# Attention and SwiGLU on one core: matrix pieces in a stored order, no order between the two banks of a PSUM tile, and a rearranged start

## The chip, the cores and the metric

The kernel runs on one core of one Trainium2 chip. The metric is device time in microseconds (us), with the reference's inputs.

Engines: PE multiplies matrices (PEld is its weight load), DVE is VectorE, ACT is ScalarE, POOL is GpSimd, SP issues most DMA. PE writes into PSUM; a PSUM bank holds 512 fp32 per partition. "Half clock" is time in which the profile shows that PE was granted half of its clock. A load "lands" when its data has arrived.

## The reference, cut to what matters

```python
# attention: 8 batches x 8 heads, 576 positions, head size 64; causal, with a decay
decay = cum[:, :, :, None] - cum[:, :, None, :]           # cum = cumsum(log(clip(f)))
scores = np.where(causal, -1e9, q @ k.T / sqrt(64) + decay)
x = softmax(scores) @ v                                   # -> 4608 tokens x 512
# feed-forward on all tokens
xn = x / sqrt(mean(x * x) + 1e-6) * rms_g
g = xn @ w_gate                                           # 512 -> 1536
out = (g * sigmoid(g) * (xn @ w_val)) @ w_out             # 1536 -> 512, fp32
```

## The kernel before

The kernel cuts all work into pieces and has a planner in Python that decides, while the program is built, in which order each engine does its pieces. The program itself is static: on the chip, each engine takes its instructions in that order and waits on semaphores. On PE the pieces are, with the letters used below: T turns queries and keys, S and L are scores, V multiplies by values, X turns the normalised result (d, once, turns the decay); then, for a group of 512 tokens, 12 gates G, 12 values U, and 8 output products P. A G and its U are four matmuls of 512 columns each, a P is six.

Before, the planner picked PE's next piece by a greedy rule:

```python
def choose(cands):                                # cuts marked by ...
    ffn = [c for c in cands if c[2].name[0] in "GUP"]
    att = sorted((c for c in cands if c[2].name[0] not in "GUP"), key=...)
    late = u + LEAD(u) - done["att"] / att_us     # how far attention is to run ahead
    ...
# a gate is made to follow the piece before it, so G and U alternate:
add(("G", g, fc), "PE", 0.87, ..., own + [("w", fc // 4 * 2)] + ([last] if last else []), [bg, ("xT", g)])
add(("U", g, fc), "PE", 0.87, ..., [("G", g, fc), ...], [bg, ("xT", g)])
last = ("U", g, fc)
```

G and U share one PSUM tile of two banks. Three such tiles (`bufs=3`) serve the scores, the G/U pairs and the outputs. ACT takes tanh of bank 0, DVE multiplies twice:

```python
def gate(g, fc):
    bg = bgs[g, fc] = ps_b.tile([128, 2, GT], F32, name="bg")
    ... nc.tensor.matmul(bg[:, 0, :], lhsT=wg[...], rhs=xTs[g][:, dc, :], ...)
def gate_tanh(g, fc):
    readers[g, fc] = [nc.scalar.activation(ths[g, fc], bgs[g, fc][:, 0, :], ACT.Tanh, scale=0.5)]
def value(g, fc):
    ... mm = nc.tensor.matmul(bgs[g, fc][:, 1, :], lhsT=wv[...], ...)
        beside(mm, readers.get((g, fc), ()))      # no dependency on readers of bank 0 that stand before it
```

The framework tracks dependencies by tile, not by bank. `beside` frees a value matmul from a tanh emitted before it. It doesn't free a tanh that is emitted after the value matmul: that tanh waits for a bank it doesn't read.

The softmax here doesn't subtract the row's maximum and nothing guards it: scores larger than these inputs give would overflow.

## Time and profile before

| | before |
|---|---|
| time, median of 4 | 441.9 us (441.7 to 446.0) |
| profiled run, span | 442.8 us |
| PE busy | 387.9 us, 88% |
| half clock | 17.1 us in three stretches |

Lines of the page of the kernel before: the busy times; then PE, ACT, granted PE clock and DMA in 40 equal slices (a digit is tenths).

```profile
PE 387.9 (88%) x3267; PEld 207.4 (47%) x3317; DVE 263.0 (59%) x545; ACT 216.9 (49%) x364; POOL 171.3 (39%) x358
...
PE   1756888879999799999999998998898999999996
...
ACT  3564644455546833675575347454682351332322
...
PEclk9986999988999999999999999999999999999999
DMA  9999999899436703583237030200011001102002
```

PE looks nearly full, but its row counts overlapped and stretched time too. I use another account: for each two neighbouring matmuls, the distance of their starts minus the distance that undisturbed ones of that size have in this trace (216 ns at 512 columns, 56 ns at 128, 29 ns at 65). What is over is lost. The undisturbed distances alone sum to 356 us.

The waits view of PE before (who waited for whom: total us, times, longest us):

```profile
PE tr L308 <- DVE qkb L286: 8.8, 3, 7.7
PE bg L575 <- ACT PT L362: 5.3, 10, 0.9
PE bg L357 <- DVE QK L314: 4.4, 7, 2.0
PE bg L442 <- DVE xn L433: 4.2, 1, 4.2
PE po L395 <- ACT PT L338: 3.8, 9, 0.8
PE po L395 <- POOL PT L323: 3.3, 5, 1.8
PE po L395 <- DVE x L406: 2.7, 5, 0.6
```

The first (the start) and fourth (the first normalisation) are single long waits. The others are many short ones: a gate (L575) that waits for an exp (L362) to free a PSUM tile, scores that wait for a QK copy, value products that wait for exps, masks and copies.

The line of the tanh in the groups view (busy us, mean ns of one | idle before it, and who ended the idle time):

```profile
L580 ACT ACTIVATE th<-bg 128x512 f32<-128x512 f32 x108 | 64.4, 597 | 120.5 <-PE bg L590 103.5 <-PE bg L575 11.7 <-PE po L334 2.3
```

L590 is the value matmul. And in the timeline (start us, duration, engine, line):

```profile
156.03 1.03 PE L575 MATMUL bg<-xT,wg 128*128 128x512 bf16 x4
...
156.89 1.03 PE L590 MATMUL bg<-xT,wv 128*128 128x512 bf16 x4
...
157.75 1.03 PE L575 MATMUL bg<-xT,wg 128*128 128x512 bf16 x4
...
157.96 0.60 ACT L580 ACTIVATE th<-bg 128x512 f32<-128x512 f32 x1 [1.13 <-PE bg L590]
```

The gate ends at 157.06 us, its value at 157.92 us, and the tanh, which reads the gate alone, starts at 157.96 us.

### The profile page before, as it was taken

Reading aid. Unit: us, or ns where it says so; the run is one execution under the profiler, and the core shown is the slowest. Engines: PE = TensorE matmul, PEld = TensorE weight load, DVE = VectorE, ACT = ScalarE, POOL = GpSimd, SP = SyncE. Lnnn points to the kernel's source line nnn. Section 1 sums busy time; section 2 is a strip of 40 time slices with the busy share of each in tenths; the row PEclk is TensorE's granted clock in tenths of the full one; section 3 lists DMA queues with packets and bytes.
Section 4 is the critical chain, followed back from the end, with each engine's and each line's share of the span. In section 5 each row is a group of like instructions: output and inputs, shape, how many; then the busy total and the mean of one; then the engine's idle time right before and its main releaser. Section 6 shows DMA issues by size and latency. Waiting matters only on the chain.

```text
span 442.8 us, 8567 instructions
## 1 busy us (share of the span) xinstructions
PE 387.9 (88%) x3267; PEld 207.4 (47%) x3317; DVE 263.0 (59%) x545; ACT 216.9 (49%) x364; POOL 171.3 (39%) x358
## 2 busy tenths in 40 slices
PE   1756888879999799999999998998898999999996
PEld 1443444545445445554545554544444444444442
DVE  5754666255763587566755784666553873670770
ACT  3564644455546833675575347454682351332322
POOL 2848545796429703862274148332330010000000
PEclk9986999988999999999999999999999999999999
DMA  9999999899436703583237030200011001102002
GB/s 158 205 198 200 202 206 212 153 248 205 90 73 155 191 1 73 143 204 73 64 83 199 1 73 2 95 2 2 1 48 49 1 0 49 48 1 80 16 0 96
DMA packets 123658, 43.19 MB, mean 98 GB/s; under 512 B 114272, under 2 KB 118880, under 8 KB 123616
## 3 DMA queue, kind: packets, MB, share of 16 engines
q1 hardware_dynamic: 118784, 37.65, 38.9%
q0 software_dynamic: 4832, 4.98, 6.8%
q8 instruction: 26, 0.43, 0.4%
q14 instruction: 16, 0.13, 0.1%
HBM read 37.90 MB, written 9.44 MB: 107 GB/s over the span
## 4 chain that ended last, share of the span: by engine, by line
PE 62%; DVE 12%; ACT 7%; DMA 5%; issue 5%; SPq 4%; POOL 4%; ACTq 0%; POOLq 0%; DVEq 0%
PE bg L575 18%; PE bg L590 17%; PE bg L606 17%; DMA v<-in_v_dram 5%; PE po L395 4%; SPq L182 4%; DVE th L584 3%; DVE hT L596 3%; DVE x L406 2%; PE bg L357 2%; ACT th L580 2%; ACT PT L362 2%; PE tr L442 2%; PE tr L308 1%; DVE xn L433 1%
## 5 line engine op out<-in xcount | busy, mean ns | idle before, releaser
L580 ACT ACTIVATE th<-bg 128x512 f32<-128x512 f32 x108 | 64.4, 597 | 120.5 <-PE bg L590 103.5
L584 DVE SCALAR_TENSOR_TENSOR th<-th,bg 128x512 f32<-128x512 f32 x108 | 74.2, 687 | 82.1 <-ACT th L580 79.4
L575 PE MATMUL bg<-xT,wg 128*128 128x512 bf16 x414 | 110.0, 381 | 8.4 <-ACT PT L362 5.3
L590 PE MATMUL bg<-xT,wv 128*128 128x512 bf16 x416 | 108.3, 379 | 0.9 <-issue 0.2
L362 ACT ACTIVATE PT<-bg 128x1024 bf16<-128x1024 f32 x96 | 93.6, 1024 | 26.0 <-PE bg L357 21.8
L606 PE MATMUL bg<-wo,hT 128*128 128x512 bf16 x416 | 97.7, 379 | 3.7 <-DVE hT L596 1.5
L323 POOL TENSOR_SCALAR_AFFINE_SELECT PT<-PT 128x256 bf16<-128x256 bf16 (+2 forms) x128 | 56.4, 450 | 73.1 <-ACT PT L362 43.6
L596 DVE SCALAR_TENSOR_TENSOR hT<-th,bg 128x512 bf16<-128x512 f32 x108 | 74.1, 686 | 5.7 <-PE bg L590 2.3
L575 PEld LDWEIGHTS <-wg 128*128 128x128 bf16 x432 | 41.2, 98 | 52.9 <-issue 11.1
L606 PEld LDWEIGHTS <-hT 128*128 128x128 bf16 x432 | 40.5, 98 | 48.1 <-issue 4.6
L590 PEld LDWEIGHTS <-wv 128*128 128x128 bf16 x432 | 40.9, 98 | 46.2 <-issue 1.0
L395 PEld LDWEIGHTS <-PT 128*128 128x128 bf16 x960 | 38.4, 101 | 22.3 <-issue 8.0
L395 PE MATMUL po<-Vs,PT 128*128 128x65 bf16 x900 | 39.9, 197 | 10.0 <-ACT PT L338 3.8
L614 ACT COPY ores<-bg 128x512 f32<-128x512 f32 x36 | 20.9, 586 | 48.3 <-PE bg L606 45.1
L357 PE MATMUL bg<-QK 64*128 64x64 bf16 (+3 forms) x576 | 33.1, 247 | 6.9 <-DVE QK L314 4.4
L314 DVE COPY QK<-tr 128x640 bf16<-128x640 bf16 (+1 forms) x64 | 28.9, 452 | 16.9 <-PE tr L308 15.7
L308 PE MATMUL tr<-ident,qkb 128*128 128x128 bf16 x288 | 28.1, 228 | 10.0 <-DVE qkb L286 8.8
L286 POOL CAST qkb<-q 128x512 bf16<-128x512 f32 x28 | 17.2, 615 | 46.8 <-PE tr L308 43.8
L293 POOL TENSOR_TENSOR Vs<-v,decT 128x512 bf16<-128x512 f32 x30 | 31.5, 1062 | 0.8 <-DMA v<-in_v_dram 0.6
L406 DVE TENSOR_TENSOR x<-po,rden 128x320 f32<-128x320 f32 x60 | 29.5, 492 | 2.1
L308 PEld LDWEIGHTS <-qkb 128*128 128x128 bf16 x288 | 20.0, 101 | 20.8 <-DVE qkb L286 9.8
L462 DVE TENSOR_SCALAR xT<-tr,rg 128x448 bf16<-128x448 bf16 (+7 forms) x58 | 18.4, 358 | 18.3 <-PE tr L442 18.2
(63 smaller groups left out, 232.5 us busy)
## 6 DMA issues: line engine op xcount, KB each, us to landing
out_dram<-ores SPq DMA_DIRECT2D x36, 256.0 KB, 2.0
q<-in_q_dram SPq DMA_DIRECT2D x64, 128.0 KB, 3.4
v<-in_v_dram SPq DMA_DIRECT2D x64, 128.0 KB, 3.5
k<-in_k_dram SPq DMA_DIRECT2D x62, 128.0 KB, 3.5
wg<-in_moe_w_gate_dram POOLq DMA_DIRECT2D x3, 512.0 KB, 6.7
wv<-in_moe_w_val_dram POOLq DMA_DIRECT2D x3, 512.0 KB, 9.3
wo<-in_moe_w_out_dram POOLq DMA_DIRECT2D x2, 768.0 KB, 10.5
r<-in_q_dram SPq DMA_DIRECT2D x8, 128.0 KB, 3.9
```

The lines of the kernel that those rows point to most:

```text
L308: nc.tensor.transpose(tp[:, (c - c0) * 128:(c - c0 + 1) * 128], src[:, c, :, :].rearrange("p h d -> p (h d)"), ident)
L323: nc.gpsimd.affine_select(out=d, in_=d, pattern=pattern, compare_op=ALU.is_ge, fill=0.0, base=0, channel_multiplier=-1)
L357: nc.tensor.matmul(sc[:, par, c:c + m], lhsT=QK[n][rows, KEYS[kj]:KEYS[kj] + 128], rhs=QK[n][rows, q0:q0 + m], start=True, stop=True)
L362: nc.scalar.activation(t[:, bank, :, :], bgs.pop((n, bank, "s")), ACT.Exp, scale=scale)
L395: mm = nc.tensor.matmul(po[:, qi, :], lhsT=weights_of(n, par, qi, kj), rhs=Vs[b % 2][:, kj, h, :], start=(kj == 0), stop=(kj == qi))
L406: nc.vector.tensor_tensor(x[:, :, h * D:(h + 1) * D], po[:, :, 0:D], bcast(r[:, :], D), ALU.mult))
L575: nc.tensor.matmul(bg[:, 0, :], lhsT=wg[:, dc, fc * 128:(fc + 1) * 128], rhs=xTs[g][:, dc, :], start=(dc == 0), stop=(dc == NDC - 1))
L580: readers[g, fc] = [nc.scalar.activation(ths[g, fc], bgs[g, fc][:, 0, :], ACT.Tanh, scale=0.5)]
L584: readers[g, fc] += [nc.vector.scalar_tensor_tensor(t, in0=t, scalar=1.0, in1=bgs[g, fc][:, 0, :], op0=ALU.add, op1=ALU.mult)]
L590: mm = nc.tensor.matmul(pv, lhsT=wv[:, dc, fc * 128:(fc + 1) * 128], rhs=xTs[g][:, dc, :], start=(dc == 0), stop=(dc == NDC - 1))
L596: nc.vector.scalar_tensor_tensor(hT, in0=ths.pop((g, fc)), scalar=0.5, in1=bgs.pop((g, fc))[:, 1, :], op0=ALU.mult, op1=ALU.mult)
L606: mm = nc.tensor.matmul(po, lhsT=hTs[g, fc][:, j * 128:(j + 1) * 128], rhs=wo[:, fc, :], start=(fc == 0), stop=(fc == NFC - 1))
```

## The change

Its intent: an order of PE's pieces found beforehand and stored as a string; the two banks of a tile made independent in both directions; a start with the first loads earlier and the exp table (what ACT loads before its first exp) fetched while DVE works. The core of the diff (`...` marks cuts):

```diff
+ORDER = "".join("""
+TTSTSSTdTLSTSSLTVTSSVSSLVVSLSVVVTVTXXXXSTGXUGGLUUTGUSGXUTGVTULSV
+... (7 lines cut)
+GUUGPPUPGPUGUGGGUUUPPPPPPPP
+""".split())
...
-        plan.run(choose, rank, count)
+        plan.run([queues[c].pop(0) for c in ORDER])
...
-    def beside(mm, others):
-        for other in others:
-            tc.declare_no_dep(mm.ins, other.ins, reason="another part")
+    def in_bank(tile, bank, *instructions):
+        for ins in instructions:
+            seen = banks.setdefault(tile, [])
+            for other_bank, other in seen:
+                if other_bank != bank and other.ins.engine != ins.ins.engine:
+                    tc.declare_no_dep(ins.ins, other.ins, reason="another bank")
+            seen.append((bank, ins))
...
-                own + [("w", fc // 4 * 2)] + ([last] if last else []), [bg, ("xT", g)])
+                own + [("w", fc // 4 * 2)], [bg, ("xT", g)])
...
+    NHT = NFC + 6                      # hidden buffers: 18, were NFC + 2 = 14
-    START_W = (14.0, 14.0, 27.5, 28.0, 36.0, 37.0, 44.0, 46.0)
+    START_W = (14.0, 14.0, 24.0, 25.0, 32.0, 33.0, 42.0, 44.0)
...
+    add("ident_f", "POOL", 1.3, rows_of_one, behind=("ld", 0, "k"))      # identity after the first key loads
+    add("tables", "ACT", 1.5, lambda: nc.scalar.activation(spare, mhalf[0:1, 0:1], ACT.Exp), ["log", "ident_f"])
+    add("gains", "SP", 0.6, load_gains, dma=0.1, behind=("ld", 3, "v"))  # gains (rms_g) later
```

The durations that the planner assumes for the other engines are renewed as well (tanh 0.63 us, was 0.60; DVE's multiply 0.72, was 0.69, and so on). They order DVE, ACT, POOL and SP around the fixed order on PE. The freedom of the banks is legal on the chip: the Trainium skill, "PSUM — Partial Sum Buffer", section "PSUM bank collisions raise a hardware error", says that two engines on different banks run clean.

## The prediction

> **What bounds the kernel now.** TensorE is busy 388 of 442.8 us (busy table), but its own work is smaller. With the start-to-start spacing of undisturbed matmuls in the trace (216 ns at 512 columns, 56 ns at 128; the Trainium skill, "TensorE: Matmul & The Clock Gate", section "Wait — 56ns, not 53.3ns?", gives 215.7 and 55.6, and the trace agrees), all pieces add up to an estimated 358 us. The other 85 us: 7.7 before the first matmul, 3.9 after the last, and time lost between matmuls: 22 us up to 40 us, 17 from 40 to 100, 40 from 100 to 380, 0.4 after that (timeline of PE). About 4.4 us of it is half clock, three stretches after idle gaps. So ordering and latency bound it, not an engine's limit: DVE is busy 59%, ACT 49%. DMA is saturated until about 82 us.
>
> **What the change does.** Matmul work is unchanged.
> 1. No order between the banks. Before, the value matmuls are emitted ahead of the tanh that reads the other bank, so tanh waits for them: the groups view gives 120 us idle before tanh, 103 released by value matmuls; the median tanh starts 0.90 us after its gate's last matmul, where one 4-matmul piece takes 0.86. After, 0.05 to 0.2 us. ACT runs in order, so exps behind it, and the PSUM buffers they free, come earlier too. FFN alone (380 to 440 us) lost only 0.4 us, so this pays only in the mixed stretch.
> 2. Stored order: attention runs further ahead (batch 1's products end at PE work 39 us, not 47; batch 2's at 80, not 87; estimates), gates run two ahead, output products are split among transposes, with 18 instead of 14 hidden buffers. This attacks the 40 us of waits spread thinly over exp, QK copies, x copies and hT.
> 3. Start: key loads before the identity, gains later, exp table (1.28 us) off the decay chain. First matmul 1 to 1.5 us earlier.
>
> **How much is critical.** Loads limit the early part: two batches (estimated 15.3 us each, from landings 0.6 us apart) and all weights (estimated 29 us) can't be in before about 61 us; batch 2's last queries and keys landed at 79 us, and the new order needs them at PE work 52 us, so at least 27 us are lost by there (before: 45). Savings, estimated: start 4 us, 40 to 100 us 7, 100 to 380 us 15 (40 to 25). Tail unchanged (eight output products end both orders).
>
> **Prediction:** 416 us, 8 in 10 between 406 and 429. Faster by over 2%: 0.92; within 2%: 0.07; slower: 0.01.
>
> **What would show it.** First matmul near 6.5 us; tanh idle released by gate rather than value matmuls, median start under 0.3 us after the gate; matmul spacing unchanged; PE busy about 375 us, its share 90% or more; lost time in the mixed stretch near 25 us; nothing gained in the last 60 us; DMA bytes equal.
>
> **What would make it wrong.** A fixed order stalls PE on whatever comes late: if batch 2's transposes stand before their loads land, PE stands with gates ready behind them, and the early gain vanishes. If two gates ahead hold all three PSUM buffers, scores wait. If DVE's pair (0.69 us twice per 1.73 us of gate and value) ends the waits rather than tanh, bank freedom gives little. If the stored order fits the chip better than I allow, it goes to 405.

## The result, and the profile after

| | before | after |
|---|---|---|
| time, median | 441.9 us | 414.3 us (413.1 to 415.5, 4 runs) |
| ratio of fast runs | | 0.935, 95% interval 0.930 to 0.941 |
| profiled run, span | 442.8 us | 411.4 us |
| PE busy | 387.9 us, 88% | 381.6 us, 93% |
| half clock | 17.1 us in three stretches | 17.1 us in two stretches |

A ratio is the mean time of one kernel's fast runs over that of the other's in the same rounds, so it isn't quite the ratio of the medians.

The same lines of the page after:

```profile
PE 381.6 (93%) x3317; PEld 204.5 (50%) x3317; DVE 263.6 (64%) x545; ACT 216.8 (53%) x365; POOL 171.9 (42%) x358
...
PE   0784977999999999999999999999999999999996
...
ACT  4575553776357644746786447744754443323221
...
PEclk9996995999999999999999999999999999999999
DMA  9999999999876531646364400200020002001002
```

From the eighth slice on PE is full. In the first four slices PE does no more than before (19 tenths of a slice in both; a slice is 11.1 us before and 10.3 us after), and in the sixth and seventh it falls to 7; the clock's dip in the seventh slice (62 to 72 us) is new. The account of lost time, worked out from the two traces as told above (us of PE time in each stretch):

```
stretch (us)      before   after
before first matmul  7.7     7.3
0 to 40             22.4    22.0
40 to 100           16.0    14.2
100 to 380          36.6     7.8
380 to the end       0.0     0.0
after last matmul    3.9     3.9
sum                 86.6    55.2      difference 31.4 = 442.8 - 411.4
```

The traces' 50 missing matmul records of the kernel before are filled in here. The stretches of the prediction (22, 17, 40) are some 4 to 5 us larger in sum; it seems that it counted a part of the missing records as lost time. With its two ends and the 0.4 us they come to 91 us, not to the 85 us that it names.

So nearly all of the gain comes from the mixed stretch, where attention and feed-forward share PE. All the lines of the waits view of PE after:

```profile
PE tr L326 <- DVE qkb L304: 9.4, 4, 7.3
PE tr L326 <- DVE QK L332: 5.8, 3, 4.4
PE tr L326 <- POOL qkb L304: 2.6, 1, 2.6
PE po L416 <- POOL PT L341: 2.3, 1, 2.3
PE tr L326 <- DVE qkb L301: 1.7, 1, 1.7
PE bg L465 <- DVE xn L456: 1.2, 1, 1.2
PE bg L378 <- DVE x L427: 0.9, 2, 0.5
PE bg L606 <- DVE hT L629: 0.8, 1, 0.8
PE bg L378 <- DVE QK L332: 0.5, 1, 0.5
PE po L416 <- DVE x L427: 0.4, 1, 0.4
```

The many short waits are gone; no gate waits for an exp any more. The tanh's line and a piece of the timeline (L606 is the gate now, L622 the value, L612 the tanh):

```profile
L612 ACT ACTIVATE th<-bg 128x512 f32<-128x512 f32 x108 | 64.5, 598 | 79.6 <-PE bg L606 79.4
```

```profile
155.86 1.89 PE L606 MATMUL bg<-xT,wg 128*128 128x512 bf16 x8
...
157.59 1.03 PE L622 MATMUL bg<-xT,wv 128*128 128x512 bf16 x4
...
157.79 0.60 ACT L612 ACTIVATE th<-bg 128x512 f32<-128x512 f32 x1 [0.27 <-PE bg L606]
```

Here two gates stand in a row (x8), and the second one's tanh starts at 157.79 us, 0.04 us after the gate's end, while the value runs. The median of all 108 tanh is 0.04 us after the gate's last matmul; it was 0.90 us.

What is left between 55 and 70 us is long waits. In the timeline after:

```profile
58.10 0.24 PE L416 MATMUL po<-Vs,PT 128*128 128x65 bf16 x2
...
58.74 1.06 POOL L311 TENSOR_TENSOR Vs<-v,decT 128x512 bf16<-128x512 f32 x1 [3.64 <-DMA v<-in_v_dram]
...
60.69 1.05 PE L416 MATMUL po<-Vs,PT 128*128 128x65 bf16 x13 [2.35 <-POOL PT L341]
...
61.55 1.90 PE L606 MATMUL bg<-xT,wg 128*128 128x512 bf16 x4
...
65.41 0.61 POOL L304 CAST qkb<-q 128x512 bf16<-128x512 f32 x1 [3.95 <-DMA q<-in_q_dram]
...
66.07 0.96 PE L326 MATMUL tr<-ident,qkb 128*128 128x128 bf16 x5 [2.63 <-POOL qkb L304]
```

POOL waits for the last values of batch 1 and for the first queries of batch 2; PE stands behind POOL, in its fixed order. Four gate matmuls take 1.90 us in place of 1.03 us: from 61.1 us on PE had half its clock for 10.2 us.

### The profile page after: what moved, and what is told of

Same layout as the page of the kernel before. It is cut to its first block, busy times and chain, and to the rows that moved or that the text cites. A ratio compares the mean times of both kernels' runs of the same rounds, so it can differ in the third digit from the quotient of the medians.

```text
span 411.4 us, 8714 instructions
## 1 busy us (share of the span) xinstructions
PE 381.6 (93%) x3317; PEld 204.5 (50%) x3317; DVE 263.6 (64%) x545; ACT 216.8 (53%) x365; POOL 171.9 (42%) x358
## 2 busy tenths in 40 slices
DMA packets 123658, 43.19 MB, mean 105 GB/s; under 512 B 114272, under 2 KB 118880, under 8 KB 123616
## 4 chain that ended last, share of the span: by engine, by line
PE 87%; DVE 4%; DMA 4%; SPq 2%; issue 1%; POOL 1%; ACT 0%; DVEq 0%; POOLq 0%; ACTq 0%
PE bg L622 22%; PE bg L639 22%; PE bg L606 22%; PE po L416 7%; PE bg L378 6%; PE tr L326 4%; DMA r<-in_k_dram 3%; PE tr L465 2%; SPq L196 1%; SPq L192 1%; DMA q<-in_q_dram 1%; DVE xn L456 1%; DVE x L427 1%; DVE junk_DVE L440 1%; DVE qkb L304 1%
## 5 line engine op out<-in xcount | busy, mean ns | idle before, releaser
L606 PE MATMUL bg<-xT,wg 128*128 128x512 bf16 x432 | 108.5, 382 | 0.8 <-DVE hT L629 0.8
L622 PE MATMUL bg<-xT,wv 128*128 128x512 bf16 x432 | 107.0, 381 | 0.0
L612 ACT ACTIVATE th<-bg 128x512 f32<-128x512 f32 x108 | 64.5, 598 | 79.6 <-PE bg L606 79.4
L639 PE MATMUL bg<-wo,hT 128*128 128x512 bf16 x432 | 101.5, 379 | 0.0
L629 DVE SCALAR_TENSOR_TENSOR hT<-th,bg 128x512 bf16<-128x512 f32 x108 | 72.5, 684 | 16.3 <-PE bg L622 9.4
L622 PEld LDWEIGHTS <-wv 128*128 128x128 bf16 x432 | 40.6, 98 | 44.9 <-issue 1.2
L606 PEld LDWEIGHTS <-wg 128*128 128x128 bf16 x432 | 40.3, 98 | 45.4 <-issue 2.5
L326 PE MATMUL tr<-ident,qkb 128*128 128x128 bf16 x288 | 29.6, 234 | 19.5 <-DVE qkb L304 9.4
L416 PEld LDWEIGHTS <-PT 128*128 128x128 bf16 x960 | 37.2, 99 | 12.4 <-POOL PT L341 2.7
L332 DVE COPY QK<-tr 128x640 bf16<-128x640 bf16 x64 | 29.0, 453 | 21.8 <-PE tr L326 16.4
L416 PE MATMUL po<-Vs,PT 128*128 128x65 bf16 x900 | 38.7, 196 | 2.8 <-POOL PT L341 2.3
L326 PEld LDWEIGHTS <-qkb 128*128 128x128 bf16 x288 | 20.9, 103 | 32.1 <-DVE qkb L304 10.2
```

The source lines that it names most:

```text
L326: nc.tensor.transpose(tp[:, (c - c0) * 128:(c - c0 + 1) * 128], src[:, c, :, :].rearrange("p h d -> p (h d)"), ident)
L416: mm = nc.tensor.matmul(po[:, qi, :], lhsT=weights_of(n, par, qi, kj), rhs=Vs[b % 2][:, kj, h, :], start=(kj == 0), stop=(kj == qi))
L606: mm = nc.tensor.matmul(bg[:, 0, :], lhsT=wg[:, dc, fc * 128:(fc + 1) * 128], rhs=xTs[g][:, dc, :], start=(dc == 0), stop=(dc == NDC - 1))
L612: in_bank(("bg", "f", g, fc), 0, nc.scalar.activation(ths[g, fc], bgs[g, fc][:, 0, :], ACT.Tanh, scale=0.5))
L622: mm = nc.tensor.matmul(pv, lhsT=wv[:, dc, fc * 128:(fc + 1) * 128], rhs=xTs[g][:, dc, :], start=(dc == 0), stop=(dc == NDC - 1))
L629: nc.vector.scalar_tensor_tensor(hT, in0=ths.pop((g, fc)), scalar=0.5, in1=bgs.pop((g, fc))[:, 1, :], op0=ALU.mult, op1=ALU.mult))
```

## The experiments

Twelve kernels ran. All outputs are right. The first four split the gain. Theory: the order is most of it. Rival: the freedom of the banks is.

### The old rule for the banks, in the stored order

```diff
-                if other_bank != bank and other.ins.engine != ins.ins.engine:
+                if other_bank != bank and other.ins.engine != ins.ins.engine \
+                        and ins.ins.engine == mybir.EngineType.PE and tile[1] != "x":
```

> The changed kernel, with the old rule for the banks (only a matmul that follows a reader of the other bank is free of it; a reader that follows a matmul of the other bank waits). In the stored order only 30 of 108 tanh stand behind their own value matmuls, in the old order 88. Theory (the order is most of it, and running gates ahead already avoids the wait): 415 to 421 us, under 2% lost. Rival (freedom of the banks is the main part): 425 us or more.

Measured: 425.3 us, ratio to the kernel before 0.957 (0.950 to 0.964). The instructions stand in the same order; only waits differ. Free banks are worth 11 us in the stored order: more than the theory allowed, and at the edge of what the rival had forecast (425 us or more). The tanh's line shows what came back:

```profile
L612 ACT ACTIVATE th<-bg 128x512 f32<-128x512 f32 x108 | 64.5, 597 | 94.2 <-PE bg L606 55.2 <-PE bg L622 37.5 <-DVE hT L629 1.4
```

A part of the idle time, 37.5 us, is again released by value matmuls. These are the waits of 30 of the 108 tanh, as many as the text above counts behind their own value matmuls.

### The old order on PE, with the rest of the change

```diff
-ORDER = (the stored order)
+ORDER = (the letters of the kernel before, in 9 lines)
+    queues["T"][0:2] = queues["T"][1::-1]      # keys of the first pair first, as before
```

> The changed kernel with exactly the old order of the pieces on PE; the free banks, the 18 hidden buffers, the new start and the new durations stay. Theory: 430 to 440 us, most of the gain is lost. Rival (free banks): 415 to 424 us.

Measured: 436.2 us, ratio 0.984 (0.978 to 0.989). The order, with what the planner makes of the other engines around it, is worth 22 us. As an account of most of the gain the rival falls: with free banks the tanh is on time here too (median 0.04 us after the gate), and still 22 of the 28 us are missing. Of the first two runs, one went to each side.

### The old order and the old rule for the banks

The two edits above together.

> The changed kernel with the old order on PE and the old rule for the banks; what is left of the change is its start, the buffers and the durations that order the other engines. Both theories: 438 to 444 us, near the kernel before. If it is under 434, the rest of the change is worth more than I think. The difference to order_old is what free banks are worth in the old order: theory 2 to 8 us, rival 15 us or more.

Measured: 449.6 us, ratio 1.014 (1.008 to 1.019), 13.4 us above the run with the old order and free banks. So in the old order free banks are worth 13 us, between the two theories' figures. It is also some 7 us slower than the kernel before, which neither theory expected. What differs from it is the start, the renewed durations and earlier weight loads, which order the other engines, and the 18 buffers. In the account of lost time the excess is in the mixed stretch (41.2 us, 36.6 before). Which of these parts costs it stays open.

### Gates not ahead of values

In the stored order, the places of G and U are kept but alternate again:

```diff
-GTUTSVGTLSUVSXGTVULSVXGVGTLGVUUUPTPSTPP...
+(the same places, each G followed by its U)
```

> The changed kernel with the same stored order, except that among the places of gates and values they alternate again (gate, its value, next gate), so that no gate runs ahead; free banks stay. Theory that running gates ahead is a large part of the gain: 422 to 432 us. Rival, that attention running ahead and the split output products are the gain: under 419 us.

Measured: 425.9 us, ratio 0.961 (0.954 to 0.968). Letting gates run ahead, with the other engines' order that comes with it, is worth 11.6 us in this order, with free banks; the mixed stretch loses 19.3 us in place of 7.8. (The planner orders the other engines around PE's order, so theirs moved too, and the two shares aren't separated. This holds for every run that changes PE's order.)

### Later loads of the output weights, first try

The next two ask why the early part gained so little. The output weights were issued at 50 and 51 us and landed at 60 and 65 us, though the first output product starts at 82 us; the queries of batch 2 landed at 62 and 65 us.

```diff
-    START_W = (14.0, 14.0, 24.0, 25.0, 32.0, 33.0, 42.0, 44.0)
+    START_W = (14.0, 14.0, 24.0, 25.0, 32.0, 33.0, 58.0, 62.0)
```

> The changed kernel with the two loads of the output weights issued later (their earliest times in the plan 58 and 62 us, not 42 and 44); nothing else. In the changed kernel they were issued at 50 and 51 us, landed at 60 and 65 us and were first needed at 82 us, while the queries of batch 2, issued from 47 us, landed only at 62 and 65 us, and PE stood 2.4 us and 4.5 us between 58 and 66 us and then ran at half clock for 10.2 us. Theory (the weight loads take the bandwidth of those queries): the queries land near 56 to 58 us, the stall before the transposes of batch 2 and most of the half clock go, 405 to 410 us. Rival (the loads of queries are late anyway, or the time is lost again later): 412 us or more.

(The 4.5 us in this text is a misreading, and so is the 6.9 us in a text further below: the two waits between 58 and 66 us are 2.4 and 2.6 us, 5.0 us together.) Measured: 422.7 us, ratio 0.955 (0.953 to 0.958): 8 us slower than the changed kernel, against the theory. This wait is new in it:

```profile
PE bg L639 <- DMA wo<-in_moe_w_out_dram: 4.4, 2, 3.6
```

It was a badly made test. The planner's 58 and 62 us became 70 and 75 us on the chip, the weights landed at 80 and 85 us, and output products waited. From 60 to 80 us, where the theory spoke, this kernel lost 2.9 us (7.7 in the changed kernel); from 80 to 100 us it lost 12.9 (1.9).

### Later loads of the last third of gate and value weights too

```diff
+    START_W = (14.0, 14.0, 24.0, 25.0, 46.0, 48.0, 60.0, 64.0)
```

> As the run before, and the last third of gate and value weights later too (46 and 48 us in the plan, not 32 and 33; they landed at 51 and 55 us and were first needed at 72 and 73 us), so that the values of batch 1 (landed at 55 and 59 us; their scaling ended the 2.4 us stall) come earlier as well. Theory: 402 to 408 us, below the run before. Rival: gates wait for their weights, or nothing changes: as the run before or slower.

Measured: 420.9 us, ratio 0.953 (0.949 to 0.956). The same fault: output weights landed at 75 and 81 us, with 5.5 us of waits on them.

### The parts of the start undone

```diff
+    rows_of_one()                               # identity before the key loads
+    with nc.allow_non_contiguous_dma(reason="512 gains, once"):
+        nc.sync.dma_start(out=rg, in_=moe_rms_g.rearrange("(c p) -> p c", p=128))
-    add("tables", "ACT", 1.5, lambda: nc.scalar.activation(spare, mhalf[0:1, 0:1], ACT.Exp), ...)
+    add("tables", "ACT", 1.5, lambda: None, ...)
     (the ops "ident_f" and "gains" keep their place in the plan and emit nothing)
```

> The changed kernel with the three parts of the start undone: identity before the key loads, gains loaded first, exp table not fetched ahead. The times of the plan are left, so that the other engines keep their order. Theory, from the trace: first matmul came only 0.35 us earlier and the first gate 1.1 us later than in the kernel before, so the start is worth at most 1 us: 413.5 to 416 us. Rival (the prediction's 4 us at the start): 417 to 419 us.

Measured: 413.9 us (409.6 to 415.1, 6 runs), ratio 0.934 (0.931 to 0.938), the same as the changed kernel. The new start is worth nothing.

### Keys first on PE

```diff
+    queues["T"][0:2] = queues["T"][1::-1]
```

> The changed kernel with the first two pieces swapped on PE: keys turned before queries, as the kernel before had it. DVE casts the keys first (6.17 us), but the stored order makes PE wait for the queries (7.35 us), and the fifth query piece waits till 9.64 us. Theory: first matmul near 6.7 us, first scores 0.5 to 1 us earlier, 0.5 to 1.5 us less in all if the start is a chain; else the same as the changed kernel within 0.5 us.

Measured: 416.0 us, ratio 0.940 (0.938 to 0.943). The first matmul came at 6.95 us and the first value products at 19.1 us in place of 20.8 us, but the first gate at 40.7 us, where it was 40.6. The gain of 1.7 us was gone again within the first batch. The text above expected a gain or the same time; that the run is 1.7 us slower is within the overlap of the two intervals. The last values of batch 1 landed at 60 and 64 us, not 55 and 59; the second third of the gate and value weights was issued earlier (at 31 and 34 us, not 36 and 39), since the planner had reordered POOL too. So the swap wasn't tested alone.

### The output weights moved, and nothing else

This repeats the failed test in a clean way: the plan is untouched, and two DMA instructions are issued later in POOL's stream.

```diff
+    MOVED = {("W", 7): 6, ("C", 8, 0): 7}       # after this piece of POOL: load weights 6, 7
...
             op.emit()
+            self.then(op.name)                  # issues the moved load
...
-        add(("w", i), "POOL", 1.0, lambda i=i: load_w(i) if i < 6 else load_wo(i - 6), ...)
+        add(("w", i), "POOL", 1.0, (lambda: None) if i in MOVED.values() else lambda i=i: ..., ...)
```

> wo_late was a bad test: by its trace the loads of the output weights were issued at 70 and 75 us, landed at 80 and 85 us, and PE waited for them (4.4 us), while up to 80 us it had done more work than the changed kernel (40.3 against 38.7 us); and a later time in the plan also reordered VectorE, ScalarE and GpSimd. Here the plan is kept as it is, and only these two loads are issued later in the stream of GpSimd: after the scaling of the last values of batch 1 and after the first query cast of batch 2. By the order of instructions nothing else moves. Theory (the weight loads delay the queries of batch 2): issued near 57 to 59 us, landing before 70 us, first needed after 74 us; the stalls between 58 and 66 us fall from 6.9 us to under 3 us, and 407 to 411 us in all. Rival (late loads are not what holds the early part): 413 us or more.

Measured: 409.6 us (406.3 to 412.2, 6 runs), ratio 0.925 (0.921 to 0.929). In its timeline the queries of batch 2 are cast at 59.16 us, not at 65.41 us, without a wait, and PE turns them without one:

```profile
59.16 0.61 POOL L307 CAST qkb<-q 128x512 bf16<-128x512 f32 x1
...
60.87 0.44 PE L329 MATMUL tr<-ident,qkb 128*128 128x128 bf16 x5
```

The queries landed at 54 and 56 us, the output weights at 65 and 71 us, before the first product at 75 us. The half clock from 61 us is gone, and 60 to 80 us loses 2.1 us in place of 7.7.

That the place of the two loads is worth some 5 us is shown by the times: nothing else was moved, and the slowest of these six runs is faster than the fastest of the changed kernel (412.2 against 413.1 us). That they cost it by holding up the queries is not shown. The queries were issued at 44.2 and 44.8 us here, and at 47.2 and 50.4 us in the changed kernel. The first of these differences can't come from the edit, since the changed kernel issues its first output weights only at 49.8 us:

```profile
47.19 4.26 SPq L192 DMA_DIRECT2D q<-in_q_dram  x2
...
49.83 0.89 POOL L220 DMA_DIRECT2D wo<-in_moe_w_out_dram  x1
```

And the trace of the run with the start undone, whose output weights stand in the old place (issued at 51.3 and 52.5 us), has the same cast at the same time, without a wait, and no half clock from 61 us either; its queries were issued at 44.4 and 47.1 us and landed at 56.1 and 56.7 us:

```profile
59.21 0.61 POOL L307 CAST qkb<-q 128x512 bf16<-128x512 f32 x1
```

Both traces are of the fastest of six runs (406.3 and 409.6 us; medians 409.6 and 413.9). So early queries come without the edit too, and one trace of each kernel can't tell how much of the picture is the edit's.

### The last gate and value weights moved as well

```diff
+    MOVED = {("C", 7, 0): 4, ("m", 5, 0): 5, ("W", 7): 6, ("C", 8, 0): 7}
```

> As the run before, and the last gate and value weights are also moved in the stream of GpSimd, to about 48 and 51 us (issued at 42.8 and 44.1 us in the changed kernel, first needed at 72 and 73 us). Theory: the values of batch 1 land before 56 us and the 2.4 us stall on their scaling goes too: 405 to 409 us, 1 to 3 us under the run before. Rival: gates or values now wait for these weights, or no difference.

Measured: 406.8 us (405.1 to 408.6, 6 runs), ratio 0.919 (0.917 to 0.922). This is the best kernel: 8.1% under the kernel before. The values of batch 1 land at 50 us. From 60 to 80 us its trace loses about 5 us, more than the trace of the run before, so single traces don't carry this comparison. Whether it beats the run before is within the spread of both.

### Free banks alone, in the kernel before

The function `in_bank` and its calls for gates, values and outputs, put into the kernel before. The order of instructions is the same on every engine.

```diff
         readers[g, fc] = [nc.scalar.activation(ths[g, fc], bgs[g, fc][:, 0, :], ACT.Tanh, scale=0.5)]
+        in_bank(("bg", "f", g, fc), 0, *readers[g, fc])
...
-            beside(mm, readers.get((g, fc), ()))
+            in_bank(("bg", "f", g, fc), 1, mm)
```

> The kernel before with only the new rule for the banks of gate, value and output tiles; by the order of instructions every engine's order is as before, only waits are gone. From order_old against both_old (436.2 and 449.6 us), free banks are worth 3% in the old order: theory 427 to 433 us, the tanh's idle time released by value matmuls gone. Rival (the 13 us there came from the new durations together with the banks): 436 us or more.

Measured: 429.0 us, ratio 0.969 (0.966 to 0.972): 13 us from removed waits alone. The tanh's line:

```profile
L591 ACT ACTIVATE th<-bg 128x512 f32<-128x512 f32 x108 | 64.5, 597 | 100.3 <-PE bg L585 96.3 <-PE po L344 1.9 <-DVE hT L610 1.6
```

The release has gone from value to gate matmuls (L585). No gate waits for an exp in it any more (5.3 us, 10 times, in the kernel before). The mixed stretch loses 25.7 us, where it lost 36.6.

### Output products together

The eight P of each group are put at the place of the first; all else of the stored order stays.

```diff
-...GTLGVUUUPTPSTPPTSTVSXPTPXPLXSVXPVSG...
+...GTLGVUUUPPPPPPPPTSTTSTVSXTXLXSVXVSG...
```

> The changed kernel with the eight output products of each group put together at the place of the first, the rest of the stored order unchanged: no attention piece and no gate stands between them. The run with alternating gates lost 11.6 us of the order's 22 us. Theory: the mixing with products is the rest, because the turned x and QK copies and exps of attention need time between pieces that only long products give: 420 to 430 us. Rival: mixing is worth nothing, and the rest is attention running ahead: under 418 us.

Measured: 444.3 us, ratio 1.008 (1.001 to 1.015). Both theories missed: this costs 30 us, more than the whole order is worth over the old one. The wait with the largest sum in it is new:

```profile
PE tr L465 <- DVE xT L487: 10.5, 15, 0.7
```

Turned pieces go through one PSUM tile (`ps_tr`, `bufs=1`). When they stand side by side, each waits for DVE to empty it; between two long products the copy is hidden. The kernel before mixed its products with attention too, so this shows that the mixing must not be lost, not what the stored order adds to it. The values of single features of an order don't add up. That attention runs further ahead, which the prediction named as well, was not tested by itself.

## Why the prediction was right or wrong

The predicted 416 us lie close to the measured 414.3 us, but this is partly luck: the sum is right with terms that are not. The mixed stretch gave 14 us more than forecast, the start and the early part 8 us less.

- **What bounds the kernel: right.** Waits and order, not an engine. PE's matmul spacing was unchanged (216 ns), and removing waits alone in the kernel before gave 3%.
- **Free banks: right in mechanism.** The tanh moved from 0.90 to 0.04 us after the gate, released by gates, and the gain lies in the mixed stretch. It is worth 13 us in the old order and 11 us in the stored one. The prediction gave no separate figure.
- **The mixed stretch, "15 (40 to 25)": the term was mis-sized.** It gave 29 us (36.6 to 7.8). I had taken 25 of 40 us to remain; cut to 100 to 380 us, the waits view after is empty; before, it had waits of a gate for an exp (2.9 us, 7 times) and sixteen more lines there.
- **"Start 4": wrong.** It gave 0.4 us before the first matmul and another 0.4 us up to 40 us, and undoing the three parts changed nothing. First, the stored order makes PE wait for queries while DVE casts keys first, so the first matmul came at 7.35 us, not 6.5. Second, an earlier start wasn't passed on: keys first brought the first value products 1.7 us forward and the first gate not at all.
- **"40 to 100 us 7": mis-sized.** It gave 1.8 us. What the prediction had named as its first risk happened: transposes of batch 2 stand in the fixed order before their loads have landed. PE waited 2.4 and 2.6 us and then ran at half clock. Moving weight loads out of the way gave 4.7 and 7.4 us (409.6 and 406.8 against 414.3), which is what the prediction's term had hoped for; by which path is open (see the run with the output weights moved). The Trainium skill, "DMA: Bandwidth & Descriptors", section "Issuing engines are not separate DMA queues", says that DMAs started by different engines run on the same 16 DMA engines and interleave. The trace agrees: queries issued at 47 us, ahead of the output weights at 50 us, landed at 62 us, behind the first of them (60 us). With these weights later, and the queries issued at 44 us, they landed at 54 us; the earlier issue is not the edit's work, so this pair of figures doesn't measure the collision.
- **"At least 27 us are lost" by PE work of 52 us: true but loose.** Even in the best kernel 39 us were lost by 100 us (7.8 before the first matmul, 31.1 after), at PE work of 61 us.
- **PE busy 375 us at 90% or more:** 381.6 us at 93%. **Last 60 us and tail:** unchanged, as predicted. **DMA:** 43.19 MB in both.

Taken in this order, the parts are: free banks 442.2 to 429.0 us (-13), the rest of the change without the order up to 436.2 us (+7), the stored order down to 414.3 us (-22). Taken the other way, with banks last: +7, -24, -11. The cause of the +7 us is not settled. With 14 or 16 hidden buffers the planner finds no way to carry out the stored order ("no piece can start"), so the larger pool is a condition of the order rather than a gain by itself.

## What to carry to other kernels

If a consumer reads one bank of a tile and a later producer writes the other, look at who ends the consumer's idle time: a release by the producer of the other bank is a false wait, and here it was worth about 3% in two orders of the pieces. When one trace is to show a cause, look first at whether a run without the change has the same picture. A fixed order on the busiest engine must respect when loads land, so weights that are needed late should be tried later, behind the loads that the order needs first (1 to 2% here); test this by moving the DMA instructions alone, since a planner that is told a new time reorders other engines as well. An earlier start was worth nothing here, since the next stage did not start earlier.

## What the Trainium skill lacked or had wrong

- "TensorE: Matmul & The Clock Gate" (section "Why this matters for your kernels") advises no PE-idle gaps over about 3 us. Here half clock began at 61.1 us in the changed kernel after a gap of 2.35 us at most in the 3.4 us before, in which PE was busy for 0.97 us; and at 96.1 us in the kernel before after a gap of 1.83 us (busy 1.44 us). What lay below half was the busy share of these 3.4 us (28% and 42%), not one long gap. Cut into stretches of 3.41 us (the half-clock stretches that end before a trace does are multiples of it), from 8 us to 4 us before the end, the 14 traces have 28 stretches at full clock with PE busy under 50%, and each was followed by half clock; of 26 with 50 to 62% five were, and none with more.
- "ScalarE: Activation LUTs" (section "What ACT_TABLE_LOAD costs") gives about 1283 ns for the load, which the trace has too (1.28 us), and 2.66 us with a drain. In the changed kernel the load starts 0.02 us after the log's end (7.67 us), and the exp behind it 1.32 us after that end, so the whole switch took 1.32 us and no drain showed. Taking this load off the chain, with the other two parts of the start, was worth nothing (413.9 against 414.3 us).
- "DMA: Bandwidth & Descriptors" says that DMAs of all issuing engines interleave, but no page gives a figure for how long small loads take among large ones: in the changed kernel 128 KB took up to 14.9 us from issue to landing beside the weight loads (median 3.4 us).
